# The second reading's range check on ScalarE instead of VectorE, in a linear-attention and SiLU kernel

## The chip, the cores and the metric

The kernel runs on one core of a Trainium2 chip, in one launch. The metric is device time in microseconds. The engines are named as in the profile: PE (TensorE, with PEld for its weight loads), DVE (VectorE), ACT (ScalarE), POOL (GpSimd) and SP (SyncE, which here only issues transfers).

## The reference

A gated recurrence over 768 tokens, for 4 batches and 8 heads of dimension 48, feeds a two-layer network with SiLU over 3072 tokens (384 to 2048 to 384):

```python
for t in range(S):
    state = alpha[:, :, t, :, None] * state + np.einsum('bhd,bhe->bhde', k[:, :, t], v[:, :, t])
    y[:, :, t] = np.einsum('bhd,bhde->bhe', q[:, :, t], state)
x = y.transpose(0, 2, 1, 3).reshape(B * S, H * D)
h = x @ w_in
out = (h * (1.0 / (1.0 + np.exp(-h)))) @ w_out
```

The two weight matrices arrive in 8-byte floats (the code tests for it with `wide`), everything else in 4-byte floats.

## The kernel before, in words

The work is in `quotients` (line 356). It takes the recurrence in 24 chunks of 128 tokens (`NT`, one batch and one stretch of tokens each) and handles it by products and quotients of the gates, which holds only while the numbers stay within a range. So it also checks its inputs. If the check fails, the program runs `general` instead (line 20), which is written at the end behind a branch (line 1267); with the inputs measured here that branch isn't taken.

**Steps and slots.** The loop at line 1185 makes 25 steps of four slots. In a slot one stage of the attention is issued: from step 8 on, slot 0 has `land` and `scores` of the chunk before (`n = step - 1`), slot 1 `products` and slot 2 `quotient` of the current one, slot 3 `values`, `states` and `flip` of the one before. After each stage `fill(step, slot)` (line 1166) issues pieces of the network by due times: `marks` names the slots at which phases of the piece list begin and end, and `fill` issues pieces until the work due by then is done. What is left after the loop is issued one piece after the other.

**Pieces.** `enter_plain` (line 897, first two groups of four chunks) makes one ps_m bank by twelve matmuls and a Silu on ACT. `enter` (line 917, the four other groups) makes the first layer by a scheme of 20 products for each of two column halves, in seven pieces; each product goes to one of three ps_m banks, and each bank is read by a copy on ACT (line 936) or a sum on DVE (line 944) before it is written again. One of the copies' targets, `part`, has a single buffer that DVE reads. `leave` (line 1021) makes the second layer in seven products of two ps_o banks, read by ACT copies (lines 1040, 1059, 1064) and DVE sums (lines 1042, 1074, 1085). From the third group on, a piece of `leave` of one group alternates with a piece of `enter` of the next. At the start of each such group `sums_x` (line 878) makes eleven sums on DVE.

**Order.** A scheduler orders each engine's instructions at build time; a call of `keep_in_program_order` pins an instruction behind the one traced just before it on its engine. PE's are all pinned from the step at which the weights have been converted. The order on the chip is then fixed, and each engine works through its queue in order, with semaphores where another engine or a transfer must be awaited.

**The check.** The weights and alpha are read a second time, for their range. `audit` (line 657) is a generator over 37 pieces: 9 of alpha (128 x 1024 floats, 512 KB), 12 of w_in (128 x 512 doubles, 512 KB) and 16 of w_out (128 x 384 doubles, 384 KB). For each it issues a transfer from SP's queue (lines 675, 677) into the single buffer `bits`, and at its next call reduces it on DVE (line 685): the largest magnitude of alpha, the largest and the smallest magnitude of the weights' upper words, 65 reduces in all. `fill` calls it in every second slot from step 15 on (line 1178); the loop at line 1215 calls it for the rest, between the last pieces. Then lines 1220 to 1239 turn the collected maxima and minima into one flag, which each engine loads.

Of the kernel before, what the change touches and what calls it, by code (L numbers as in the profile page):

```python
# [8 lines left out]
F32 = mybir.dt.float32  # L9
I32 = mybir.dt.int32  # L10
U32 = mybir.dt.uint32
U8 = mybir.dt.uint8
AF = mybir.ActivationFunctionType
ALU = mybir.AluOpType
E = mybir.EngineType
AX = mybir.AxisListType.X
# [3 lines left out]
def general(  # L20
# [89 lines left out]
    for i, L in enumerate(LEVELS):  # L110
        top = work.tile([128, 128], I32, name="top")
        dve.tensor_single_scalar(top, xor, i, ALU.logical_shift_right)
        right = top.rearrange("p (b two l) -> p b two l", two=2, l=L)[:, :, 1, :]
        m = masks[L] = consts.tile([128, NP, 64], U8, name=f"mask{L}")
        for j in range(NP):
# [18 lines left out]
    def weights():  # L134
# [8 lines left out]
        for dst, src in pieces:  # L143
# [15 lines left out]
            m = gpool.tile([128, 512], F32, name="g")[:, 0:n]  # L159
            act.activation(m, top, AF.Copy, bias=1.0, scale=2.0**-20)  # L160
            dve.scalar_tensor_tensor(m, lo, 2.0**-52, m, ALU.mult, ALU.add)
# [116 lines left out]
    def moe(ci):  # L278
# [3 lines left out]
        for f in range(NFT):  # L282
# [4 lines left out]
            gf = gpool.tile([128, B * C], F32, name="g")  # L287
            act.activation(gf, ps, AF.Silu)
            gs.append(gf)
# [66 lines left out]
def quotients(  # L356
# [19 lines left out]
    nc = tc.nc  # L376
    dve, act, gps = nc.vector, nc.scalar, nc.gpsimd
# [16 lines left out]
    B, H, S, D = q.shape  # L394
# [3 lines left out]
    HD = H * D  # L398
    DF = moe_w_in.shape[1]
    NKT = HD // 128  # L400
    NFT = DF // 128
# [3 lines left out]
    GB = 4  # L405
# [6 lines left out]
    def pool(name, bufs=1, space=None):  # L412
        kw = {} if space is None else {"space": space}
        return ctx.enter_context(tc.tile_pool(name=name, bufs=bufs, **kw))

    PS = bass.MemoryType.PSUM
    consts = pool("consts")
    fix = pool("fix")
# [21 lines left out]
    dve.memset(table, 0.0)  # L440
    act.activation(table, table, AF.Silu)
    ident = consts.tile([128, 128], F32, name="ident")
# [64 lines left out]
    wide = moe_w_in.dtype != F32  # L507
    pieces_in = [(t, c) for c in range(0, DF, 512) for t in range(NKT)]
    sources = [moe_w_in[t * 128 : t * 128 + 128, c : c + 512] for t, c in pieces_in]
# [44 lines left out]
    earlier, later = [(low, 0), (high, 1)], [(low, 1), (high, 0)]  # L554
    ones = consts.tile([128, 1], F32, name="ones")
    gps.memset(ones, 1.0)

    st = [fix.tile([128, NP, 2, D], F32, name=f"st{b}") for b in range(B)]
    for t in st:
# [54 lines left out]
    def weights(which):  # L614
# [9 lines left out]
        def rounding(bits):  # L624
# [3 lines left out]
            tc.keep_in_program_order(  # L628
                act.activation(up, bits.bitcast(U32)[:, :, 0], AF.Copy, scale=2.0**-29))
            return up  # L630
# [21 lines left out]


    AW = 1024
    seen = []

    def audit():


        flat = alpha.rearrange("b h s d -> (b h s d)").rearrange("(p c) -> p c", p=128)  # L660
        todo = [(flat[:, c : c + AW], AW, 0) for c in range(0, flat.shape[1], AW)]
        if wide:
            todo += [(moe_w_in[t * 128 : t * 128 + 128, c : c + 512], 512, 1)
                     for c in range(0, DF, 512) for t in range(NKT)]
            todo += [(moe_w_out[f * 128 : f * 128 + 128, :], HD, 1) for f in range(NFT)]
        for kind in (0, 1):
            n = sum(x[2] == kind for x in todo)
            if n:
                seen.append([fix.tile([128, n], F32, name=f"seen{kind}{i}") for i in range(2)])
        at = [0, 0]  # L670
        for src, n, kind in todo:
            t = late["look"].tile([128, 512, 2], I32, name="bits")
            if kind == 0:
                x = t.rearrange("p n w -> p (n w)")[:, 0:n].bitcast(F32)
                nc.sync.dma_start(x, src)
            else:
                nc.sync.dma_start(t[:, 0:n, :].rearrange("p n w -> p (n w)"), src.bitcast(I32))
                x = t[:, 0:n, 1]
            yield
            i = at[kind]  # L680
            at[kind] += 1
            for which, op in ((0, ALU.max), (1, ALU.min)):
                if kind == 1 or which == 0:
                    tc.keep_in_program_order(
                        dve.tensor_reduce(seen[kind][which][:, i : i + 1], x, axis=AX, op=op,  # L685
                                          apply_absolute_value=True))

    xts, xcs = {}, {}

# [207 lines left out]
    def enter_plain(grp, h, pair):  # L897
# [4 lines left out]
        for f in range(8 * pair, 8 * pair + 8, 2):  # L902
# [5 lines left out]
            q, i = divmod(f, 4)  # L908
            act.activation(gts[grp, h, pair][:, i : i + 2, q % 2, :], ps, AF.Silu)  # L909
            if grp == 1 and pair == h == 0:  # L910
# [6 lines left out]
    def enter(grp, pair):  # L917
# [21 lines left out]
        def silu(h, i):  # L939
            x = halves[h][:, i : i + 2]  # L940
            act.activation(x, x, AF.Silu)  # L941

# [156 lines left out]
    def convert(which, upto):  # L1099
        while conv_done[which] < min(upto, n_conv[which]):  # L1100
            next(conv[which], None)
            conv_done[which] += 1
# [38 lines left out]
    def go_on():  # L1141

        nonlocal done
        next(pieces[done][0], None)
        done += 1

    audits = audit()
    done, bridged = 0, 0
    STEPS = NT + 1
# [16 lines left out]
    def fill(step, slot):  # L1166

        at = step * SLOTS + slot
        if at < marks[0]:
            if at == SLOTS:  # L1170
                next(conv[0])
            elif step >= 1:
                convert(0, (at - SLOTS) * 3 // (marks[0] - SLOTS) + 1)
            return
        i = next(i for i, m in enumerate(marks[1:]) if at < m)
        a, b = [work_at[n] for n in ([0] + phases)[i : i + 2]]
        due = a + (b - a) * (at - marks[i] + 1) / (marks[i + 1] - marks[i])
        if at % 2 == 0 and step > 3 * GB + 2:
            next(audits, None)
        while work_at[done + 1] <= due and pieces[done][2] <= bridged:  # L1180
            convert(0, 3 * (done // 2) + 6)
            convert(1, 3 * (done - 6) // 2)
            go_on()

    for step in range(STEPS):
        if step == 1:
            load(NIN)
        stages = [[(scores, 1)], [(products, 0)], [(values, 1)], [(states, 1)]]
        if step == 1:

            stages = stages[1::-1] + stages[2:]
        elif step >= NA:
            stages = [[(land, 1), (scores, 1)], [(products, 0)], [(quotient, 0)],
                      [(values, 1), (states, 1), (flip, 0)]]
        for slot, group in enumerate(stages):
            for stage, lag in group:
                n = step - lag
                if not 0 <= n < NT:
                    continue
                stage(n)  # L1200
                if stage is values:
                    bridged = n + 1
                if stage is states and n + 1 + NIN < NA:
                    load(n + 1 + NIN)
                if stage is states and n + NV < NT:
                    load_v(n + NV)
            if step * SLOTS + slot == (NA + 1) * SLOTS - 1:
                x = decayed.rearrange("p (o i c) -> p o i c", o=2, c=C)
                for r, o in later:
                    gps.memset(x[r, o, :, 0:CH], 0.0)  # L1210
            fill(step, slot)
            if step * SLOTS + slot >= NA * SLOTS - 1 and conv_done[1] == NFT and not late:
                settle()
    turns = 0
    while next(audits, 0) is None:
        turns += 1
        for _ in range(1 + turns % 2):
            go_on()

    checks = [(least.rearrange("p n j -> p (n j)"), ALU.min, 2.0**-64, ALU.is_gt),  # L1220
              (seen[0][0], ALU.max, 1.0, ALU.is_le)]
    if wide:
        checks += [(seen[1][0], ALU.max, float(1083 << 20), ALU.is_le),
                   (seen[1][1], ALU.min, float(898 << 20), ALU.is_ge)]
    ends = work.tile([128, len(checks)], F32, name="ends")
    for i, (x, op, bound, holds) in enumerate(checks):
        e = ends[:, i : i + 1]
# [21 lines left out]
@with_exitstack  # L1249
def kernel(  # L1250
    ctx: ExitStack,
    tc: tile.TileContext,
    q: bass.AP,
    k: bass.AP,
    v: bass.AP,
    alpha: bass.AP,
    moe_w_in: bass.AP,
    moe_w_out: bass.AP,
    out: bass.AP,
):  # L1260


    flag = ctx.enter_context(tc.tile_pool(name="flag", bufs=1))
    small = flag.tile([1, 1], I32, name="small")
    args = (q, k, v, alpha, moe_w_in, moe_w_out, out)
    within = quotients(tc, small, *args)
    with tc.If(within < 1, label="general"):
        general(tc, *args)
# [30 lines left out]
```

## Time and profile before

| | |
|---|---|
| median of three runs | 560.08 us (558.29, 560.08, 560.13) |
| span of the profiled execution | 558.1 us |
| mean granted TensorE clock | 0.994 |
| reduces of the check (L685) | 65, 42.5 us of DVE, first at 247.2 us, last at 518.4 us |
| transfers of the check | 37, 17.2 MB, the first of them issued at 95.3 us, the others from 248.7 to 514.8 us |
| loading of the flag (L1239) | at 527 us on four engines, at 531.8 us on PE |

The span runs from the first to the last instruction of one profiled execution; the page gives no other time for it. Busy times are shares of that span. A row of the page's fifth part names line, engine and operation, then what is written from what is read, the number of instructions, busy time and the mean of one, and last the engine's idle time just before them and what ended it. In the timeline each row has its start and its duration in us, and in brackets the idle time before it. A matmul of 4-byte floats leaves two records, so that one product of `enter` has four.

### The profile page before, as it was taken

Reading aid. Unit: us, or ns where it says so; the run is one execution under the profiler, and the core shown is the slowest. Engines: PE = TensorE matmul, PEld = TensorE weight load, DVE = VectorE, ACT = ScalarE, POOL = GpSimd, SP = SyncE. Lnnn points to the kernel's source line nnn. Section 1 sums busy time; section 2 is a strip of 40 time slices with the busy share of each in tenths; the row PEclk is TensorE's granted clock in tenths of the full one; section 3 lists DMA queues with packets and bytes.
Section 4 is the critical chain, followed back from the end, with each engine's and each line's share of the span. In section 5 each row is a group of like instructions: output and inputs, shape, how many; then the busy total and the mean of one; then the engine's idle time right before and its main releaser. Section 6 shows DMA issues by size and latency. Waiting matters only on the chain. (4 is left out here: it accounts for less than half of the span.)

```text
span 558.1 us, 12640 instructions
## 1 busy us (share of the span) xinstructions
PE 541.4 (97%) x5026; PEld 488.8 (88%) x5026; DVE 445.1 (80%) x801; ACT 208.4 (37%) x466; POOL 75.9 (14%) x146
## 2 busy tenths in 40 slices
PE   5999999999999999999999999999999999999996
PEld 3788887998899898899999999988998999998996
DVE  5887889974999799997998986998894775857531
ACT  3456643223333243353353353353263341432200
POOL 4100010221211211021021021021121000001000
PEclk9799999999999999999999999999999999999999
DMA  9999861164445525355445654717712122333101
GB/s 218 255 276 177 232 189 40 38 164 108 126 131 136 142 62 134 88 145 157 129 109 142 194 141 115 198 22 179 180 48 84 53 99 95 111 109 106 38 25 32
DMA packets 99220, 70.13 MB, mean 126 GB/s; under 512 B 56272, under 2 KB 88656, under 8 KB 99152
## 3 DMA queue, kind: packets, MB, share of 16 engines
q1 hardware_dynamic: 97232, 65.30, 44.6%
q0 software_dynamic: 1920, 3.93, 2.0%
q8 instruction: 41, 0.67, 0.5%
q14 instruction: 27, 0.22, 0.1%
HBM read 61.34 MB, written 7.86 MB: 124 GB/s over the span
## 5 line engine op out<-in xcount | busy, mean ns | idle before, releaser
L388 PE MATMUL ps_o<-w_out,g 128*128 128x192 f32 x768 | 134.7, 329 | 1.1 <-DVE o L1042 0.9
L388 PEld LDWEIGHTS ps_o<-w_out,g 128*128 128x128 f32 x768 | 125.4, 190 | 5.1 <-DVE o L1042 2.3
L388 PE MATMUL ps_m<-xt,w_in 128*128 128x256 f32 x480 | 113.6, 383 | 1.5 <-ACT xt L851 1.1
L388 PEld LDWEIGHTS ps_m<-xt,w_in 128*128 128x128 f32 x480 | 89.1, 190 | 14.4 <-ACT xt L851 1.6
L388 PE MATMUL ps_o<-wt,g 128*128 128x192 f32 x576 | 99.7, 326 | 0.0
L388 PEld LDWEIGHTS ps_o<-wt,g 128*128 128x128 f32 x576 | 95.1, 190 | 1.6 <-issue 0.2
L388 PE MATMUL ps_m<-xc,w_in 128*128 128x256 f32 x288 | 70.7, 382 | 0.0
L685 DVE TENSOR_REDUCE seen<-bits 128x1 f32<-128x384 int32 (+2 forms) x65 | 42.5, 689 | 24.0 <-DMA bits<-in_moe_w_out_dram 19.6
L388 PEld LDWEIGHTS ps_m<-xc,w_in 128*128 128x128 f32 x288 | 53.6, 190 | 7.0 <-DVE g L944 0.3
L941 ACT ACTIVATE g<-g 128x1024 f32<-128x1024 f32 x32 | 33.0, 1056 | 59.0 <-DVE g L944 59.0
L1033 DVE TENSOR_TENSOR g<-g 128x512 f32<-128x512 f32 x72 | 49.8, 708 | 6.1 <-PE ps_o L388 6.1
L1045 POOL DMA_DIRECT2D out_dram<-o x40 | 22.0, 550 | 223.2 <-DVE o L1042 127.6
L813 POOL TENSOR_SCALAR_AFFINE_SELECT g<-g 64x256 f32<-64x256 f32 x64 | 34.2, 534 | 124.8 <-ACT g L806 105.8
L388 PE MATMUL ps_m<-xc,wx 128*128 128x256 f32 x192 | 50.0, 383 | 1.0 <-DVE xc L586 1.0
L936 ACT COPY g<-ps_m 128x512 f32<-128x512 f32 x64 | 36.5, 588 | 36.5 <-PE ps_m L388 36.4
L388 PEld LDWEIGHTS ps_m<-xc,wx 128*128 128x128 f32 x192 | 35.2, 190 | 5.3 <-ACT u L1064 1.3
L944 DVE TENSOR_TENSOR g<-ps_m,g 128x512 f32<-128x512 f32 x56 | 37.0, 684 | 2.9 <-PE ps_m L388 2.7
L722 DVE TENSOR_TENSOR_SCAN u<-al,one 128x516 f32<-128x516 f32 x24 | 30.0, 1249 | 10.6 <-ACT al L719 10.3
L909 ACT ACTIVATE g<-ps_m 128x512 f32<-128x512 f32 x32 | 19.1, 596 | 42.8 <-PE ps_m L388 42.3
L936 ACT COPY part<-ps_m 128x512 f32<-128x512 f32 x32 | 18.9, 589 | 43.0 <-DVE g L944 21.3
L752 DVE TENSOR_TENSOR_SCAN p<-al,inv 128x516 f32<-128x516 f32 x24 | 29.9, 1246 | 1.0 <-PE ps_a L388 0.4
L388 PE MATMUL ps_a<-g,vn 128*32 128x128 f32 x768 | 27.5, 278 | 1.8 <-POOL g L801 1.7
(126 smaller groups left out, 611.4 us busy)
## 6 DMA issues: line engine op xcount, KB each, us to landing
bits<-in_moe_w_in_dram SPq DMA_DIRECT2D x24, 512.0 KB, 4.8
bits<-in_moe_w_out_dram SPq DMA_DIRECT2D x32, 384.0 KB, 3.1
at<-in_alpha_dram SPq DMA_DIRECT2D x64, 96.0 KB, 2.5
kt<-in_k_dram SPq DMA_DIRECT2D x64, 96.0 KB, 2.5
qt<-in_q_dram SPq DMA_DIRECT2D x64, 96.0 KB, 2.6
bits<-in_alpha_dram SPq DMA_DIRECT2D x9, 512.0 KB, 3.8
out_dram<-o POOLq DMA_DIRECT2D x40, 96.0 KB, 2.4
flips<-turn SPq DMA_DIRECT2D x12, 256.0 KB, 2.4
```

The source lines that it names most:

```text
L388: in_order(nc.tensor.matmul(*args, **kw))
L685: dve.tensor_reduce(seen[kind][which][:, i : i + 1], x, axis=AX, op=op, apply_absolute_value=True))
L722: dve.tensor_tensor_scan(u[:, end - 1 :: -1], sg[:, end:0:-1], one[:, end:0:-1], 0.0, ALU.mult, ALU.add)
L752: dve.tensor_tensor_scan(p[:, 0:end], sg[:, 0:end], iv[:, 0:end], 0.0, ALU.mult, ALU.add)
L813: gps.affine_select(x, x, pattern=[[0, NP], [1, CH]], compare_op=ALU.is_ge, fill=0.0, base=0, channel_multiplier=-1)
L909: act.activation(gts[grp, h, pair][:, i : i + 2, q % 2, :], ps, AF.Silu)
L936: act.copy(to, ps)
L941: act.activation(x, x, AF.Silu)
L944: dve.tensor_tensor(to, a, b, op)
L1033: dve.tensor_tensor(cells(grp, h, pair, *to), cells(grp, h, pair, *x), cells(grp, h, pair, *y), ALU.subtract)
L1045: (gps if grp < NG - 1 else nc.sync).dma_start(out[r : r + C, c * HO : (c + 1) * HO], o)
```

## The change

The check's arithmetic goes from DVE to ACT, its transfers go from SP's queue to ACT's, and its calls begin with step 10 and come twice in each slot: once before the slot's pieces and once after them. Each piece takes two calls. In the first (after the slot's pieces) Abs is made of the piece that was fetched; for a weight it reads the uppermost two bytes of each double as an integer. In the second (before the next slot's pieces) Relu is made of what exceeds the bound and is summed along the row into one column of `beyond`; for a weight another Abs stands ahead of it. Then the next transfer is issued. All of these are pinned in program order, and the buffer stays single. With two calls a slot the generator ends within the steps, so that the loop over the rest has nothing to do, and the flag is formed from `beyond` right after the last step.

```diff
+    minus = consts.tile([128, 1], F32, name="minus")
+    gps.memset(minus, -1.0)
...
     AW = 1024
-    seen = []
+    audited = [(0, c, AW) for c in range(0, B * H * S * D // 128, AW)]
+    if wide:
+        audited += [(1, src, src.shape[1]) for src in list(sources)]
+    beyond = fix.tile([128, len(audited)], F32, name="beyond")
 
     def audit():
         flat = alpha.rearrange("b h s d -> (b h s d)").rearrange("(p c) -> p c", p=128)
-        todo = [(flat[:, c : c + AW], AW, 0) for c in range(0, flat.shape[1], AW)]
...
-        for src, n, kind in todo:
+
+        def step(to, x, func, scale=1.0, bias=0.0, to_sum=None):
+            kw = {} if to_sum is None else {"accum_out": to_sum}
+            tc.keep_in_program_order(act.activation(to, x, func, bias=bias, scale=scale, **kw))
+
+        def begin(kind, src, n):
             t = late["look"].tile([128, 512, 2], I32, name="bits")
+            words = t.rearrange("p n w -> p (n w)")
+            to, src = (words[:, 0:n].bitcast(F32), flat[:, src : src + n]) if kind == 0 else (
+                words[:, 0 : 2 * n], src.bitcast(I32))
+            tc.keep_in_program_order(act.dma_start(to, src))
+            return t
+
+        t = begin(*audited[0])
+        yield
+        for i, (kind, _, n) in enumerate(audited):
+            x = t.bitcast(F32)
+            x = x.rearrange("p n w -> p (n w)")[:, 0:n] if kind == 0 else x[:, 0:n, 0]
             if kind == 0:
-                x = t.rearrange("p n w -> p (n w)")[:, 0:n].bitcast(F32)
-                nc.sync.dma_start(x, src)
+                step(x, x, AF.Abs)
             else:
-                nc.sync.dma_start(t[:, 0:n, :].rearrange("p n w -> p (n w)"), src.bitcast(I32))
-                x = t[:, 0:n, 1]
+                step(x, t.bitcast(I16)[:, 0:n, 3], AF.Abs, scale=2.0**-14)
             yield
-            i = at[kind]
-            at[kind] += 1
-            for which, op in ((0, ALU.max), (1, ALU.min)):
-                if kind == 1 or which == 0:
-                    tc.keep_in_program_order(
-                        dve.tensor_reduce(seen[kind][which][:, i : i + 1], x, axis=AX, op=op,
-                                          apply_absolute_value=True))
+            if kind == 1:
+                step(x, x, AF.Abs, scale=-1.0, bias=ones)
+            step(x, x, AF.Relu, scale=1.0 if kind == 0 else 2.0**14 / 944, bias=minus,
+                 to_sum=beyond[:, i : i + 1])
+            if i + 1 < len(audited):
+                t = begin(*audited[i + 1])
+            yield
...
-        if at % 2 == 0 and step > 3 * GB + 2:
+        if step > 2 * GB + 1:
             next(audits, None)
         while work_at[done + 1] <= due and pieces[done][2] <= bridged:
             convert(0, 3 * (done // 2) + 6)
             convert(1, 3 * (done - 6) // 2)
             go_on()
+        if step > 2 * GB + 1:
+            next(audits, None)
...
-              (seen[0][0], ALU.max, 1.0, ALU.is_le)]
-    if wide:
-        checks += [(seen[1][0], ALU.max, float(1083 << 20), ALU.is_le),
-                   (seen[1][1], ALU.min, float(898 << 20), ALU.is_ge)]
+              (beyond, ALU.max, 0.0, ALU.is_le)]
```

More of the change, by code (lines that the diff above doesn't have):

```diff
@@ L12 @@
 U8 = mybir.dt.uint8
+I16 = mybir.dt.int16
 AF = mybir.ActivationFunctionType
@@ L654, in quotients @@
     AW = 1024
-    seen = []
+    audited = [(0, c, AW) for c in range(0, B * H * S * D // 128, AW)]
+    if wide:
+        audited += [(1, src, src.shape[1]) for src in list(sources)]
+    beyond = fix.tile([128, len(audited)], F32, name="beyond")
     def audit():
         flat = alpha.rearrange("b h s d -> (b h s d)").rearrange("(p c) -> p c", p=128)
-        todo = [(flat[:, c : c + AW], AW, 0) for c in range(0, flat.shape[1], AW)]
-        if wide:
[L663 to L670, printed above, removed]
-        for src, n, kind in todo:
-            t = late["look"].tile([128, 512, 2], I32, name="bits")
+        def step(to, x, func, scale=1.0, bias=0.0, to_sum=None):
+            kw = {} if to_sum is None else {"accum_out": to_sum}
+            tc.keep_in_program_order(act.activation(to, x, func, bias=bias, scale=scale, **kw))
+        def begin(kind, src, n):
+            t = late["look"].tile([128, 512, 2], I32, name="bits")
+            words = t.rearrange("p n w -> p (n w)")
[8 more added lines that the diff above has]
+            x = x.rearrange("p n w -> p (n w)")[:, 0:n] if kind == 0 else x[:, 0:n, 0]
@@ L1220, in quotients @@
     checks = [(least.rearrange("p n j -> p (n j)"), ALU.min, 2.0**-64, ALU.is_gt),
-              (seen[0][0], ALU.max, 1.0, ALU.is_le)]
-    if wide:
-        checks += [(seen[1][0], ALU.max, float(1083 << 20), ALU.is_le),
-                   (seen[1][1], ALU.min, float(898 << 20), ALU.is_ge)]
+              (beyond, ALU.max, 0.0, ALU.is_le)]
     ends = work.tile([128, len(checks)], F32, name="ends")
```

## The prediction

> **What bounds the kernel now.** I read the page's busy times and slices first, then the waits, then busy time by stretch, then the timeline.
>
> ```profile
> span 558.1 us, 12640 instructions
> PE 541.4 (97%) x5026; PEld 488.8 (88%) x5026; DVE 445.1 (80%) x801; ACT 208.4 (37%) x466; POOL 75.9 (14%) x146
> PE   5999999999999999999999999999999999999996
> DVE  5887889974999799997998986998894775857531
> ACT  3456643223333243353353353353263341432200
> L685 DVE TENSOR_REDUCE seen<-bits 128x1 f32<-128x384 int32 (+2 forms) x65 | 42.5, 689 | 24.0 <-DMA bits<-in_moe_w_out_dram 19.6
> ```
>
> PE never rests except in the first and last slices. The range check costs DVE 42.5 us of work and 24.0 us of waiting, but DVE isn't what sets the end: what it gives up is worth only the PE gaps that it causes.
>
> ```profile
> 144.00:188.00 44.00, 44.00 (x476) 39.85 (x479) 40.41 (x74) 13.66 (x42) 9.17 (x16) 1.00 0.53 143
> 188.00:240.00 52.00, 50.65 (x577) 45.62 (x569) 50.76 (x99) 21.09 (x54) 7.71 (x15) 1.00 0.39 102
> 240.00:325.00 85.00, 85.00 (x872) 78.14 (x871) 78.17 (x128) 36.40 (x85) 13.23 (x26) 1.00 0.52 142
> ```
>
> These are the stretches that take the new work (stretch and its length, then busy us and instructions of PE, PEld, DVE, ACT, POOL). The code makes two calls per slot from step 10; 37 pieces need 75 calls, so the check runs from slot 40 to slot 77. In the trace the score matmuls start step 10 at 143.9 us and step 19 at 320.5 us. A slot lasts 4.05 us up to 188 us (16.2 us a step), then about 5.35. ACT is busy 71.2 of 181 us there; DVE has 1.2 us to spare in 52 from 188 to 240, where no check runs yet.
>
> ```profile
> 237.42 1.99 PE L388 MATMUL ps_m<-xc,w_in 128*128 128x256 f32 x8
> ...
> 240.22 1.08 ACT L936 COPY g<-ps_m 128x512 f32<-128x512 f32 x2
> ...
> 242.71 1.03 PE L388 MATMUL ps_m<-xc,wx 128*128 128x256 f32 x4
> ...
> 243.78 0.59 ACT L936 COPY part<-ps_m 128x512 f32<-128x512 f32 x1 [0.55 <-PE ps_m L388]
> ...
> 247.90 1.89 PE L388 MATMUL ps_m<-xc,w_in 128*128 128x256 f32 x8
> ```
>
> This shows how late ACT may be. Three ps_m banks go round. The bank written at 242.71 is copied at 243.78 and free at 244.37, and written again at 247.90: 3.5 us to spare. The one written at 237.42 is copied only at 240.22 (the scores' copies and L824 are ahead in ACT's queue), free at 240.81, rewritten at 242.71: 1.9 us to spare. Putting each copy of the eight entry blocks beside the next write of its bank, I find 1.7 to 2.7 us to spare in most cases for the six copies of pieces 1 and 2 of seven, and some 3.5 us or more later.
>
> **What the Trainium skill says.** "ScalarE: Activation LUTs", section "Table sets: the hidden batching unit", says that relu, copy and abs are in every set; so Abs and Relu between Silus need no table load. The trace has one load (1.28 us) for Copy and Silu together, and no Abs or Relu. The same page, "What ACT_TABLE_LOAD costs", puts an ACTIVATE at 186 ns + 0.833 ns an element, and 93 ns more for a bias given as a column; the trace agrees: 588 ns for 512 elements (L936; 613 by the formula), 1056 for 1024 (L941; 1039). "DMA: Bandwidth & Descriptors", "Issuing engines are not separate DMA queues": queues share the same DMA engines, so ACT's own queue saves only issue time, here 327 ns a piece on SP.
>
> **The change, part by part.**
>
> *Reduces leave DVE* (-42.5 us of DVE). What that is worth on PE:
>
> ```profile
> 513.75 1.00 DVE L685 TENSOR_REDUCE seen<-bits 128x1 f32<-128x384 int32 x2
> ...
> 515.68 0.76 PE L388 MATMUL ps_o<-w_out,g 128*128 128x192 f32 x3 [0.71 <-DVE o L1042]
> ```
>
> Two reduces stand ahead of the sum (L1042) that PE waits for: 0.71 us. The other gap of size after 240 us is 1.02 us at 368.7, behind an xc sum (L586), with 1.2 us of reduces at 356.8 ahead of it in a DVE queue that hardly rests in between; with two gaps of 0.12 and 0.07 the sum is **-1.9 us**. Bounds: 0 (something else is next) and -3, if the matmul starts also close up a little inside stretches shown as busy.
>
> *Transfers leave SP* (37 x 0.33 = 12 us of issue, and 85 us of SP waiting for reduces). Behind them stand the a, k, q loads and the flips; the only wait on such a load is 1.5 us of DVE, once, not on PE. Nothing, at most -1.
>
> *ACT's new work.* Alpha, 9 pieces: Abs 1.06 (row L941) and Relu with a column bias 1.15 = 2.21 us. w_in, 12: the nearest strided read is L629 at 686 ns for 512 elements; 0.69 + 0.78 + 0.78 = 2.25. w_out, 16: L629 at 564 ns for 384; 0.56 + 0.65 + 0.65 = 1.87. Sum 19.9 + 27.0 + 29.9 = 76.8 us, and 37 issues of 0.33 = 12.2: 89 us; ACTs in a row start some 0.1 us before the end of the last (240.22 to 241.18: 0.48 us apart at 0.59 each), so about 79. Reading out the accumulator isn't in the trace: 0 to 0.2 us each (the smallest ACT row takes 0.2), so 0 to 7; I take 0. ACT goes from 71 to 150 busy us of 181 (83%), before any wait.
>
> *The added wait.* A piece's Abs waits for its transfer with all later ACT work queued behind it: bank copies, which PE needs, and the part copies, which DVE needs.
>
> ```profile
> bits<-in_moe_w_in_dram SPq DMA_DIRECT2D x24, 512.0 KB, 4.8
> bits<-in_moe_w_out_dram SPq DMA_DIRECT2D x32, 384.0 KB, 3.1
> ...
> bits<-in_alpha_dram SPq DMA_DIRECT2D x9, 512.0 KB, 3.8
> ```
>
> Landing takes 3.1 to 4.8 us; the slot's pieces between issue and Abs fill 4 to 5.35. DVE, in the same position now, waited 24.0 us in 18 times, 1.3 each. I take 0.65, bounds 0 and 1.3.
>
> *What PE feels.* The slot's last Abs and the next slot's Abs, Relu and issue stand side by side on ACT, except where scores or values come between. One block is 2.25 + 0.33 - 0.2 = 2.4 us for w_in and 1.87 + 0.33 - 0.2 = 2.0 for w_out; with the wait 3.05 and 2.65. Where 3.5 us are to spare nothing shows; where 1.8 are, in 2 of 7 pieces (0.29), PE stalls 1.25 and 0.85. Entry blocks begin at about 190 us (slot 52), so 9 w_in and 16 w_out pieces meet them: 9 x 0.29 x 1.25 + 16 x 0.29 x 0.85 = 3.3 + 3.9 = **+7.2 us**. The alpha pieces and three of w_in lie beside plain pieces, each of which uses one bank for twelve matmuls of 0.216 us from start to start, 2.6 us, so that two others pass before a bank comes up again: over 4 us to spare after its Silu. 0; without that cover their blocks would cost as w_in's do. Bounds: wait 0 gives 9 x 0.29 x 0.6 + 16 x 0.29 x 0.2 = 2.5; wait 1.3 gives 5.0 + 7.0, and 9 x 0.71 x 0.2 = 1.3 in the other pieces: 13.3.
>
> *The end.* The verdict is taken once the steps are over instead of at 527 us; its DVE operations are under 1.5 us in all and PE's read of the flag took 0.48 at 531.8 without a PE gap. 0, from -0.2 to +1.
>
> Sum: 558.1 - 1.9 + 7.2 = 563.4. The page gives the span only; the runs shown were 558.29, 560.08 and 560.13, so the median lies 2.0 above the span. **565.4 us**; own range 561 to 572.
>
> **Rivals.**
> *ACT's idle time takes it all* (not slower). For it: ACT idles 110 us in these stretches, 59 us of all its idling is waiting for DVE (first line below), which gets quicker, and placement may put the blocks into those waits. Against: the order is fixed, and DVE at 98% from 188 to 240 gets no relief there. It decides if a block with its wait stays under 1.8 us where copies are late. 558.1 - 1.9 + 2.0 = 558.2; 556 to 562.
>
> ```profile
> ACT g L941 <- DVE g L944: 59.0, 16, 6.4
> ...
> DVE seen L685 <- DMA bits<-in_moe_w_out_dram: 19.6, 14, 2.5
> ...
> DVE seen L685 <- DMA bits<-in_moe_w_in_dram: 4.4, 4, 1.5
> ```
>
> *ACT sets the pace.* One buffer makes a serial loop: block, landing, block. It takes 2.4 + 3.8 + 0.1 = 6.3 us for alpha, 7.3 for w_in, 5.2 for w_out. If one piece per slot really binds, slots stretch: 9 x 2.25 + 3 x 3.25 + 9 x 1.95 + 0 = 47 us, giving 605; the compiler may let the check slip against the pieces, so half: 584 (572 to 606). Against it: nothing forces later copies to stay behind a waiting Abs at build time.
>
> *It isn't what it says:* a table load for each function after all, two at 1.28 us per piece, 95 us: 650.
>
> **Chances.** Forecast 0.54 (of it 0.08 below 562.9), ACT absorbs 0.30 (0.06 of it below 557.3), ACT paces 0.14, table loads 0.02. Half a per cent, 2.8 us, is about what a measurement can tell from no change. Faster 0.06; same 0.24 + 0.08 = 0.32; slower 0.62. Range 557.5 to 582: it leaves out the fast tail (0.06) and most of the pacing case (0.12).
>
> **What would show it.** Right: no new table load; ACT near 280 to 290 us busy; new PE gaps of about 1 us between 190 and 330 us released by ACT copies or by DVE sums that wait for copies; the gaps at 368 and 515 gone; ACT waits for the new transfers under 1.3 us each. Wrong if PE shows no more gaps than now (ACT absorbed it), or if slots between 144 and 240 us stretch by 2 us each (ACT paces).

## The result and the profile after

| | before | after |
|---|---|---|
| median | 559.84 us (558.29 to 560.13) | 598.21 us (596.54 to 599.78) |
| ratio, with its 95% interval | | 1.0688 [1.0662, 1.0715] |
| span of the profiled execution | 558.1 us | 598.0 us |
| mean granted TensorE clock | 0.994 | 0.971 |

The change makes the kernel 6.9% slower; the prediction had 565.4 us and a range up to 582. Span, engines, three rows of slices (PE, ACT, PEclk) and the row of the check, from the page of the changed kernel:

```profile
span 598.0 us, 12667 instructions
PE 555.5 (93%) x5026; PEld 498.1 (83%) x5026; DVE 410.7 (69%) x732; ACT 272.6 (46%) x589; POOL 76.3 (13%) x147
PE   6999999999979769979988989999999999999996
...
ACT  3565653223556465576667555335343342332100
PEclk9999999999979779979999998999999999999999
L668 ACT ACTIVATE bits<-bits 128x384 f32<-128x384 int16 (+2 forms) x33 | 24.0, 728 | 65.1 <-DMA bits<-in_moe_w_out_dram 26.9
```

PE has the same 5026 matmul records. Its idle time went from 558.1 - 541.4 = 16.7 us to 598.0 - 555.5 = 42.5, and the matmuls themselves take 14.1 us longer: 25.8 + 14.1 = 39.9, the whole difference of the spans. The PE row now has holes in slices 12 to 24, just where ACT is fuller, and the PEclk row has its 7s there too. And ACT, which is busy for less than half of the span, stands idle for 65.1 us ahead of the check's first Abs. From slice 26 on the rows of PE and PEclk are as before: the loss is local.

Busy time by stretch of the changed kernel (stretch and length, then busy us and instructions of PE, PEld, DVE, ACT, POOL, then granted clock, DMA share, GB/s). The bounds are the score matmuls that open steps 10, 13, 15 and 19, except that two of step 15's 32 score matmuls run at 256.40 already, ahead of a gap of 3.21 us, so that this gap counts to the second stretch:

```profile
142.30:205.10 62.80, 54.17 (x568) 48.28 (x568) 45.77 (x85) 32.85 (x68) 8.70 (x16) 0.89 0.63 172
205.10:260.00 54.90, 45.95 (x435) 40.11 (x434) 43.90 (x85) 33.17 (x72) 6.59 (x12) 0.93 0.59 167
260.00:357.70 97.70, 89.09 (x863) 79.19 (x863) 70.75 (x121) 63.12 (x145) 12.49 (x24) 0.97 0.55 158
357.70:598.00 240.30, 232.16 (x1763) 215.65 (x1762) 138.36 (x245) 81.27 (x172) 24.31 (x44) 0.99 0.14 38
```

The same steps of the kernel before:

```profile
143.90:192.50 48.60, 48.60 (x569) 44.16 (x570) 44.45 (x83) 14.53 (x43) 9.17 (x16) 1.00 0.53 140
192.50:236.60 44.10, 42.75 (x435) 38.38 (x435) 43.50 (x84) 17.54 (x41) 6.21 (x12) 1.00 0.36 96
236.60:320.50 83.90, 83.90 (x865) 77.08 (x864) 78.00 (x129) 35.35 (x82) 12.23 (x24) 1.00 0.53 146
320.50:558.10 237.60, 230.89 (x1763) 214.20 (x1762) 167.61 (x310) 78.80 (x167) 24.59 (x44) 1.00 0.34 96
```

So the three stretches with the check lose 14.2, 10.8 and 13.8 us, together 38.8, and the fourth 2.7. Step by step the ten steps from 10 to 19 took 198.0 us and now take 240.7, 42.7 more; what comes ahead of them and after them is 1.6 and 1.2 us shorter. ACT is busy for only 52 to 65% of the three stretches. It isn't full; it is waiting.

What ACT waits for between 140 and 362 us in the changed kernel (us in total, times, longest):

```profile
ACT bits L668 <- DMA bits<-in_moe_w_out_dram: 26.9, 14, 3.5
ACT bits L668 <- DMA bits<-in_alpha_dram: 21.2, 8, 3.9
ACT bits L668 <- DMA bits<-in_moe_w_in_dram: 16.9, 8, 3.9
```

Thirty waits for a landing, 65.0 us in all, 2.2 each. PE's four largest waits in the same stretch:

```profile
PE ps_m L389 <- ACT g L944: 7.5, 2, 4.7
PE ps_m L389 <- ACT g L917: 4.2, 1, 4.2
PE ps_m L389 <- ACT part L944: 4.0, 6, 1.7
PE ps_a L389 <- DMA kn<-flips: 4.0, 1, 4.0
```

With the smaller rows it waits for 28.4 us: 20.5 are put down to ACT, 3.9 to sums of DVE, 4.0 to a load of the flips. How ACT's waits reach PE is seen around one of them. From the timeline of the changed kernel (start, duration, in brackets the idle time before and what ended it):

```profile
165.64 0.33 ACTq L675 DMA_DIRECT2D bits<-in_alpha_dram  x1
...
166.91 1.17 ACT L832 ACTIVATE st<-st,least 128x96 f32<-128x96 f32 x4
170.70 1.06 ACT L668 ACTIVATE bits<-bits 128x1024 f32<-128x1024 f32 x1 [2.62 <-DMA bits<-in_alpha_dram]
...
171.78 0.60 ACT L917 ACTIVATE g<-ps_m 128x512 f32<-128x512 f32 x1
...
172.43 1.65 PE L389 MATMUL ps_m<-xt,w_in 128*128 128x256 f32 x3 [4.15 <-ACT g L917]
```

The transfer begins at 165.64 and lands five microseconds later. ACT has nothing else ahead of the Abs after 168.1, so it stands for 2.62 us. The Silu that empties the bank PE needs (L917) is queued behind the Abs. PE has stopped at 168.28 and starts again at 172.43. This is a plain piece (six products, which leave twelve records), where the prediction put the cost at zero.

One thing of the change was misread in the prediction: the second reading now takes 33 pieces, not 37. The change builds its list from `sources`, and four entries of w_in have been taken from that list by then, by the fetches that run ahead. So there are 9 pieces of alpha, 8 of w_in and 16 of w_out (HBM reads 61.34 MB before, 59.24 after), and the other four of w_in aren't checked.

### The profile page after: what moved, and what is told of

The parts are those of the page before. It is cut to its first block, busy times and chain, and to the rows that moved or that the text cites. A ratio compares the mean times of both kernels' runs of the same rounds, so it can differ in the third digit from the quotient of the medians.

```text
span 598.0 us, 12667 instructions
## 1 busy us (share of the span) xinstructions
PE 555.5 (93%) x5026; PEld 498.1 (83%) x5026; DVE 410.7 (69%) x732; ACT 272.6 (46%) x589; POOL 76.3 (13%) x147
## 3 DMA queue, kind: packets, MB, share of 16 engines
HBM read 59.24 MB, written 7.86 MB: 112 GB/s over the span
## 5 line engine op out<-in xcount | busy, mean ns | idle before, releaser
L389 PEld LDWEIGHTS ps_o<-w_out,g 128*128 128x128 f32 x768 | 127.6, 192 | 5.3 <-ACT g L949 1.7
L389 PE MATMUL ps_m<-xt,w_in 128*128 128x256 f32 x480 | 116.2, 389 | 6.4 <-ACT g L917 4.2
L389 PEld LDWEIGHTS ps_m<-xt,w_in 128*128 128x128 f32 x480 | 90.5, 193 | 21.0 <-ACT g L917 4.4
L389 PE MATMUL ps_m<-xc,w_in 128*128 128x256 f32 x288 | 74.4, 396 | 0.0
L389 PE MATMUL ps_m<-xc,wx 128*128 128x256 f32 x192 | 53.3, 402 | 10.4 <-ACT g L944 7.5
L389 PEld LDWEIGHTS ps_m<-xc,w_in 128*128 128x128 f32 x288 | 55.9, 198 | 7.6 <-issue 0.2
L668 ACT ACTIVATE bits<-bits 128x384 f32<-128x384 int16 (+2 forms) x33 | 24.0, 728 | 65.1 <-DMA bits<-in_moe_w_out_dram 26.9
L389 PEld LDWEIGHTS ps_m<-xc,wx 128*128 128x128 f32 x192 | 36.9, 201 | 17.6 <-ACT g L944 8.0
L949 ACT ACTIVATE g<-g 128x1024 f32<-128x1024 f32 x32 | 32.9, 1053 | 35.9 <-DVE g L952 35.4
L952 DVE TENSOR_TENSOR g<-g,part 128x512 f32<-128x512 f32 x24 | 16.5, 686 | 30.8 <-ACT part L944 20.9
L389 PEld LDWEIGHTS ps_a<-p,kp 48*64 48x64 f32 (+1 forms) x640 | 21.4, 149 | 15.2 <-issue 7.9
L389 PE MATMUL ps_a<-p,kp 48*64 48x64 f32 (+2 forms) x640 | 26.4, 263 | 7.4 <-ACT xt L859 3.4
L917 ACT ACTIVATE g<-ps_m 128x512 f32<-128x512 f32 x32 | 18.9, 594 | 29.3 <-PE ps_m L389 28.4
```

The source lines that it names most:

```text
L389: in_order(nc.tensor.matmul(*args, **kw))
L668: tc.keep_in_program_order(act.activation(to, x, func, bias=bias, scale=scale, **kw))
L952: dve.tensor_tensor(to, a, b, op)
```

## The experiments

**Theory: one serial loop.** With a single buffer the order is: block on ACT, transfer, landing, block on ACT. ACT can't pass a waiting Abs, so when one piece per slot is called for, the loop is longer than the slot and everything that PE needs of ACT falls behind. **Rivals:** ACT's added work (some 79 us) is what delays the copies; the check's transfers, now crowded into 210 us, delay the loads that attention needs; the transfers on ACT's queue hold up SP.

### The work alone, and the wait alone

*The work alone* (e4_work_only): all of ACT's new operations, at the same places, on a resident tile; no transfer.

```diff
-            t = late["look"].tile([128, 512, 2], I32, name="bits")
+            t = late["bits"]
...
-            tc.keep_in_program_order(act.dma_start(to, src))
```

> All of ScalarE's range-check arithmetic stays where the change puts it, but it works on one resident tile and the 33 transfers are left out, so that nothing is awaited (the data are thus not checked). If the wait for the landing, with ScalarE's queue behind it, is the cause: 558 to 567 us. If ScalarE's added work alone is the cause: 585 us or more. If the transfers' traffic is the cause: 558 to 567 us as well.

Measured: 559.90 us, ratio to before 0.9975 [0.9966, 0.9984]; span 557.4 us. The engines, from its page:

```profile
PE 539.6 (97%) x5026; PEld 487.1 (87%) x5026; DVE 411.7 (74%) x732; ACT 271.1 (49%) x589; POOL 78.8 (14%) x148
```

ACT is as busy as in the change (271.1 us against 272.6) and DVE as light, and PE is as dense as before. So the work costs nothing that shows; together with DVE's relief and the missing transfers it is worth 0.25%, 1.4 us.

*The wait alone* (e3_wait_only): the transfers stay whole, the arithmetic is done on 8 columns of each piece.

```diff
+            m = 8
+            x = x[:, 0:m]
...
-                step(x, t.bitcast(I16)[:, 0:n, 3], AF.Abs, scale=2.0**-14)
+                step(x, t.bitcast(I16)[:, 0:m, 3], AF.Abs, scale=2.0**-14)
```

> All 33 transfers and the waits for them stay, but Abs and Relu take 8 columns instead of 384 to 1024 (only those are checked). If the wait for the landing is the cause, most of the loss stays: 580 to 598 us. If the added ScalarE work is the cause: 558 to 567 us. If both are needed together: 567 to 580 us.

Measured: 592.12 us, 1.0567 [1.0537, 1.0598]. ACT is busy for 230.3 us only. PE's largest wait between 140 and 362 us:

```profile
PE ps_a L389 <- DMA kn<-flips: 11.5, 3, 5.9
```

With most of the arithmetic gone, ACT only waits longer: 33.5 us for w_out, 30.9 for alpha, 26.1 for w_in, together 90.5 in 33 waits. 5.7 of the 6.9% remain. Work and wait can't be added up: without most of the work the wait gets longer. But PE's gaps have a second releaser here, the landing of `kn<-flips`, a load on SP's queue that attention needs. So the traffic and SP's queue had to be tried by themselves.

### The traffic

*Halves from SP, arithmetic on other data* (e5_traffic_no_wait): each piece is fetched in two halves from SP's queue, and ACT works on a tile that lies there already, so it waits for nothing.

```diff
-            tc.keep_in_program_order(act.dma_start(to, src))
-            return t
+            for e in range(2):
+                m = n // 2
+                to, x = ...
+                nc.sync.dma_start(to, x)
+            return late["still"]
```

> The same bytes are moved at the same points of the program, by SyncE's queue and in halves into a smaller buffer that nobody reads; ScalarE does its arithmetic on a resident tile (the data are thus not checked). Traffic and ScalarE work stay, the wait of ScalarE for the landing goes. If that wait is the cause: 558 to 568 us. If the traffic slows the loads and the flips that the steps need: 580 us or more. If the added work is the cause: 585 us or more.

Measured: 583.66 us, 1.0418 [1.0369, 1.0467], in the range named for the traffic. But this isn't a test of the traffic alone: with one buffer each half has to wait on SP for the last one to land. From SP's and PE's waits of this kernel:

```profile
SPq L677 <- DMA bits<-in_moe_w_out_dram: 30.6, 28, 2.6
```

```profile
PE ps_a L389 <- DMA kn<-flips: 17.4, 5, 6.8
```

With w_in (23.8 us) and alpha (15.1) SP waits 69.5 us for its own halves. I had moved the serial loop to SP, not removed it; what stands behind it there is the load of the flips.

*The same traffic without the loop* (e6_traffic_dram): every piece is copied, from ACT's queue as in the change, into a DRAM tile of its own that nobody reads; ACT works on a resident tile.

```diff
-            t = late["look"].tile([128, 512, 2], I32, name="bits")
+            t = aside.tile([128, 512, 2], I32, name=f"aside{len(made)}")
...
-            return t
+            return late["bits"]
```

> ScalarE's arithmetic on a resident tile as in the run with the work alone (559.9 us), and the 33 transfers of the change at their places on ScalarE's queue, each into a memory tile of its own in DRAM, so that neither ScalarE nor the queue waits for one to land (the data are thus not checked). The traffic is there in full. If the wait for the landing is the cause of nearly all: 560 to 568 us, some us over the work alone. If the traffic, which delays the flips and the loads, is the cause of a good part: 575 us or more.

Measured: 565.71 us, 1.0066 [1.0036, 1.0097]. Work and traffic together cost 0.7%, that is 0.9% more than the work alone. PE's only waits of size on this kernel's loads are two for the flips, 3.9 us in all. SP's own transfers wait 43.0 us, in 18 waits, for the landing of these copies, though nobody reads what they write; more on this below. The target is DRAM, so the bytes take another way than in the change; as a size for the traffic it is a stand-in.

### Whose queue, whose engine

*The transfers on SP's queue* (e7_sp_queue), otherwise the change:

```diff
-            tc.keep_in_program_order(act.dma_start(to, src))
+            nc.sync.dma_start(to, src)
```

> The change with one part undone: the transfers are issued on SyncE's queue again. ScalarE still waits for the landing. If the wait is the cause: 590 to 605 us, as the change or more, since SyncE now waits with its loads queued behind for ScalarE's last read of the buffer. If sharing of the queues (flips beside check transfers) matters more: 575 to 590 us.

Measured: 599.03 us, 1.0669 [1.0634, 1.0704]: no different from the change. ACT waits for landings as long (63.1 us), while PE's gaps have another releaser: 28.9 us in 7 for `kn<-flips`, which now stand on SP behind transfers that wait for ACT to empty the buffer.

*DVE's reduces with the change's calls* (e9_dve_calls): the kernel before, with its reduces and its transfers from SP, but two calls in each slot from step 10.

```diff
+            yield
...
-        if at % 2 == 0 and step > 3 * GB + 2:
+        if step > 2 * GB + 1:
             next(audits, None)
...
+        if step > 2 * GB + 1:
+            next(audits, None)
```

> The kernel before with the change's calls alone: reduces on VectorE and SyncE's queue as before, but begun from step 10, the transfer issued before a slot's pieces and reduced after them. If a wait for the landing in any engine's ordered queue is the cause, it is as slow as the change or slower, VectorE having less idle time: 595 us or more. If it is ScalarE that can't wait: 560 to 575 us.

Measured: 599.50 us, 1.0658 [1.0614, 1.0703]. With no instruction of the check on ACT the kernel loses the same 6.6%. The road isn't the one I had in mind, though. DVE waits for landings only 15.1 us between 140 and 362. Who waits on PE and on SP in that stretch:

```profile
PE ps_a L388 <- DMA kn<-flips: 30.9, 8, 6.8
```

```profile
SPq L677 <- DVE seen L685: 29.6, 16, 7.4
```

Here the loop's waiting is done by SP: the next transfer waits there for the reduce of the last piece, with the flips behind it (29.6 us for weights, 14.6 for alpha). Three kernels with two calls a slot, one buffer and the whole check (the change, e7, e9) come out between 1.066 and 1.069; the engine and the queue only decide by which way the waiting reaches PE.

*The wait with no transfer* (e12_pool_wait): in place of the transfer GpSimd writes the buffer four times, some 4 us in all. ACT waits as in the change, nothing is fetched, and SP has no part in it.

```diff
-            tc.keep_in_program_order(act.dma_start(to, src))
+            for _ in range(4):
+                tc.keep_in_program_order(gps.memset(words.bitcast(F32), 1.0))
```

> The change with its 33 transfers replaced by four fills each of the same buffer on GpSimd, about 3.8 us in all by the 0.95 us of one such fill (the data are thus not checked). ScalarE waits as long as for a landing, but nothing is transferred and SyncE has no check transfer to wait for. If ScalarE's wait with its queue behind it is enough: 585 us or more. If most of the loss comes by way of SyncE, whose loads and flips wait for the check's transfers: 560 to 570 us.

Measured: 596.25 us, 1.0629 [1.0606, 1.0651]. Waits of ACT and of PE between 140 and 362 us:

```profile
ACT bits L668 <- POOL bits L676: 78.2, 31, 4.1
```

```profile
PE ps_m L389 <- ACT g L945: 8.1, 4, 3.7
PE ps_a L389 <- ACT xt L860: 4.7, 3, 2.0
```

ACT's waiting, without the check's traffic and without SP, is enough for a loss of nearly this size, and most of PE's gaps come from ACT's copies, none from loads. Two things keep the sizes from being the same: ACT waits longer than in the change (78.2 us against 65.0), and GpSimd's own mask (L822) comes late behind its fills, so that PE waits 3.5 us for it.

### The length and the frequency of the loop

*A shorter landing* (e13_short): the transfers bring 16 of 128 partitions; ACT works on the whole tile, which lies there.

```diff
-            tc.keep_in_program_order(act.dma_start(to, src))
+            tc.keep_in_program_order(act.dma_start(to[0:16], src[0:16]))
```

> The change with each transfer cut to 16 of the 128 partitions (the others are not checked); ScalarE's work and the wait stay, the landing gets shorter, some 2.4 us by the 64 to 96 KB transfers of the profile. If the loop of block, landing and block sets the pace: 2.4 + 2.4 + 0.1 = 4.9 us against slots of 4.05 and 5.35, so 9 x 0.85 = 8 us and 3 us for w_in in short slots, together 565 to 572 us. If any wait at all costs as much: 585 us or more.

Measured: 565.36 us, 1.0083 [1.0063, 1.0104]. The median landing falls from 3.6 to 4.3 us to 2.2 to 2.6, and with 1.4 to 1.7 us less a piece the loss falls from 6.9 to 0.8%. (An eighth of the bytes is moved, too, but e6 puts all of the traffic at under 1%.) ACT's waits for landings between 140 and 362 us are 17.1 us in 11. So the loss has an edge: where the loop fits into the slot, or its excess into what ACT can slip, PE hardly feels it.

*Only the first call in each slot* (e2_one_call; a piece takes two slots):

```diff
-        if step > 2 * GB + 1:
-            next(audits, None)
```

> The change with the second call of each slot left out, so that a transfer has a whole slot with its attention stage (some 5 us) instead of the slot's pieces alone, and a piece of the check takes two slots. If the time to land decides: between the two runs measured, 562 to 572 us, with waits of ScalarE of under 1 us each. If the halved number of transfers decides: 575 to 580 us, half the loss of the change.

Measured: 562.59 us, 1.0037 [1.0023, 1.0052]. The waits weren't under 1 us each, as expected: ACT still waits 36.5 us for landings, in 18 waits, over half of what it does in the change. That costs PE next to nothing; with two slots for a piece, some 10 us from one to the next, ACT has time to catch up. Waits in themselves aren't the cost; a loop longer than the slot is.

*One call in every second slot* (e2_far): a call makes Abs and Relu of the piece and begins the next transfer, which then has two slots to land.

```diff
             else:
                 step(x, t.bitcast(I16)[:, 0:n, 3], AF.Abs, scale=2.0**-14)
-            yield
...
-        if step > 2 * GB + 1:
+        if at % 2 == 0 and step > 2 * GB + 1:
             next(audits, None)
...
-        if step > 2 * GB + 1:
-            next(audits, None)
```

> The whole check with its arithmetic on ScalarE, but a piece is worked on in one call every second slot: a transfer has two slots, about 10 us, to land instead of the pieces of one slot. If the wait for the landing is the cause: 558 to 567 us, with waits of ScalarE for these transfers near 0. If the added work as such is the cause: 570 to 590 us, since the same work is spread over twice the slots. If the traffic is the cause: about 575 us.

Measured: 562.83 us, 1.0041 [1.0028, 1.0054]. ACT's waits for landings are down to some 9 us. What is left over is on SP's side. From SP's waits of this kernel between 140 and 362 us:

```profile
SPq L487 <- DMA bits<-in_moe_w_in_dram: 15.1, 4, 5.3
```

With alpha and the flips' own loads behind it, 43 us in all: attention's loads on SP stand still until the check's transfers land, though they read and write other tiles.

*The same with the transfers on SP's queue* (e8_far_sp): the edits of e2_far and of e7_sp_queue.

> As the run with one call every second slot (562.8 us), but with the transfers on SyncE's queue, in line with the flips and loads. If what is left of its loss is the flips' landing beside a transfer of the other queue: 559 to 561.5 us. If SyncE's own waiting for ScalarE's last read takes its place: 563 us or more.

Measured: 559.18 us, 0.9962 [0.9953, 0.9970], span 557.8 us, and on its page:

```profile
PE 539.5 (97%) x5026; PEld 488.4 (88%) x5026; DVE 413.7 (74%) x732; ACT 271.5 (49%) x589; POOL 77.5 (14%) x147
```

It is faster than both kernels, by 0.4% than the one before. The waits of attention's loads for the check's transfers are down to 2.7 us between 140 and 362 us, and ACT's waits for landings are 8.6 us in all. SP waits 38.1 us for ACT to empty the buffer, without a gap on PE.

*The same with all 37 pieces* (e10_far_sp_full): the source list in full, so that the four pieces which the change leaves out are read as well.

```diff
-        audited += [(1, src, src.shape[1]) for src in list(sources)]
+        audited += [(1, moe_w_in[t * 128 : t * 128 + 128, c : c + 512], 512) for t, c in pieces_in]
+        audited += [(1, moe_w_out[f * 128 : f * 128 + 128, :], HD) for f in range(NFT)]
```

> The quicker version (one call every second slot, transfers on SyncE's queue, 559.2 us) with the four pieces of w_in put back that the change no longer reads: 37 pieces, the rest of them between the last pieces of the network. If its gain is VectorE's relief: 558.5 to 560 us, still below the kernel before. If it comes from the four pieces left out: 561 us, as the kernel before.

Measured: 559.65 us, 0.9967 [0.9956, 0.9979]. The gain of 0.3% doesn't come from reading less.

## Why the prediction was wrong

**The loop, from the trace.** All 33 transfers of the changed kernel stand in one view, that of line 675 (duration shortest/median/longest in ns, then the first and the last start):

```profile
L675 ACTq DMA_DIRECT2D bits<-in_moe_w_out_dram x16: 334/335/378, 263.2 to 354.5; - x16
L675 ACTq DMA_DIRECT2D bits<-in_alpha_dram x9: 334/334/2238, 144.3 to 200.5; - x9
L675 ACTq DMA_DIRECT2D bits<-in_moe_w_in_dram x8: 334/338/369, 206.4 to 256.5; - x8
...
DMA to landing us min/median/max: 3.0/4.0/6.6
```

From one alpha transfer to the next it is (200.5 - 144.3) / 8 = 7.0 us, of w_in 7.2, of w_out 6.1. Thirty-two turns take 354.5 - 144.3 = 210.2 us. The 32 slots that they belong to, 40 to 72, took 300.0 - 143.9 = 156.1 us in the kernel before: 54 us too few. Of these, ACT gave 18: the check slipped against the attention's slots (the first transfer starts 2.0 us after slot 40 opens, the last 20.4 us after slot 72), nearly all of it within the alpha pieces, 18.1 us by the ninth. From there on the two run in step: 154.0 us for the next 24 turns, 151.7 for the next 24 slots, where the kernel before took 123.7. So 36 us reached PE by slot 72, and 7 more in the two steps in which the slipped pieces run: the 42.7 us of the ten steps.

Point by point:

**"Reduces leave DVE", -1.9.** Right in size: e4, with the work moved and no transfers, gains 0.25%, 1.4 us; e10, with all 37 transfers, gains 0.33%; and the part of the change after step 19 is 1.2 us shorter.

**"ACT's new work".** Right. By the prediction's prices 33 pieces are 67.8 us; by the rows of each shape they are 67.5. The read-out of the sum, taken as 0 with a bound of 7 us, is an instruction of its own, with this row among those by shape:

```profile
L668 ACT ACTIVATION_READ_ACCUMULATOR bits<-bits,minus 128x1 f32 x33 | 6.3, 190 | 0.0
```

Together 73.8 us, of which 64.2 show as busy, since neighbours overlap by about 0.1. There is one table load, as before: the rival "It isn't what it says" is out, and what the Trainium skill says of relu, copy and abs ("ScalarE: Activation LUTs", "Table sets: the hidden batching unit") agrees with this trace.

**"The added wait", 0.65 us, bounds 0 and 1.3.** Measured 2.2 us in 30 of 33. The bound came from DVE's waits in the old kernel, where a piece has two slots, 10 to 11 us, for its round; in the change it has one. A block of 2.4 us and a landing of 3.8 don't fit into a slot of 4.05: the wait had to be over 2 us, from figures that the prediction itself has in its rival "ACT sets the pace".

**"What PE feels", +7.2, bounds 2.5 and 13.3.** This is the step that failed: PE got 25.8 us more of gaps, not 7.2. It laid each block, once, beside the slack of one ps_m bank, as if ACT were on time again at the next. In a loop that is longer than the slot the lateness is carried on: ACT slipped once by some 18 us, and after that nearly all of each turn's excess went to PE: from the ninth alpha piece on, 24 turns took 30.3 us more than their slots had before, and these slots took 28.0 more. So the alpha pieces, put at 0 because plain pieces have over 4 us to spare, weren't covered either (the gap of 4.15 us above is one), and the first stretch lost 14.2 us. e12 shows that ACT's waiting is enough for a loss of this kind without the check's traffic or SP, and e4 that the work without the waiting costs nothing.

**"ACT sets the pace".** The right mechanism, with a chance of 0.14. Its full loop, with the 33 pieces that there are, gives 9 x 2.25 + 3 x 3.25 + 5 x 1.95 + 16 x 0 = 39.8 us and a span of 598 us, the one that was measured; but that is in good part luck, since the turns were taken too short (alpha 6.3 for 7.0, w_out 5.2 for 6.1, so that w_out seemed to fit its slot) and neither the slip nor the slower clock is in it. Landings were 4.2 and 3.6 us in the medians for the 3.8 and 3.1 that it took, and the read-out adds 0.2. Half of it was taken off because "nothing forces later copies to stay behind a waiting Abs at build time". The order as built does put them behind it, and gave way by two pieces only: between two copies of `values` (L859) ACT's trace has three pieces of the check twice where e4's has four. Without the pins on the check's arithmetic the program has the same order on every engine (it was built, not run), so these pins aren't what holds it.

**"Transfers leave SP", 0.** Wrong in kind, and small in the change by what PE shows of it. In 24 places a transfer on SP waited for the landing of one of the check's, 88.1 us in all; the largest of SP's rows for it between 140 and 362 us in the changed kernel:

```profile
SPq L487 <- DMA bits<-in_moe_w_out_dram: 31.2, 9, 5.2
```

These load tiles that the check has nothing to do with (`at`, `kt`, `qt`), and the kernel before has 3.9 us of such waits. In the trace at 163.15 a load of `qt` waits for, and then posts, the very semaphore that ACT's transfer of 159.01 had posted. PE saw at most 4.0 us of it directly, one late landing of the flips. Waits of this kind come to 43 to 47 us in e2_far, e6 and e2_one_call as well, and these lose 0.4 to 0.7%. e2_far against e8_far_sp gives the price at a cadence where ACT's loop doesn't bind: 1.0041 against 0.9962, 0.8%. The Trainium skill's "DMA: Bandwidth & Descriptors" ("Issuing engines are not separate DMA queues"), on which the step leaned, says that a second issuing engine saves issue time only. These runs show no other gain (e7 loses 6.7%, the change 6.9%), and they show that it can also cost.

**"The end", 0.** Right, within the 1.2 us.

**Not in the prediction at all: the clock.** 14.1 of the 39.9 us are matmul time, not gaps. The granted clock right after the gap of 168.28 to 172.43 us, from the changed kernel's trace (stretch, length, PE busy, granted clock, DMA share, GB/s):

```profile
168.28:172.43 4.15, 0.00 (x0) 0.75 0.56 204
172.43:176.43 4.00, 4.00 (x9) 0.50 0.72 195
176.43:180.43 4.00, 4.00 (x97) 0.91 0.63 196
```

PE comes back at a clock of 0.50 and has its full clock again some 5 us later. The mean clocks give about as much, 598.0 x (1 - 0.971) - 558.1 x (1 - 0.994) = 14.0 us, though a part of that falls into the gaps themselves. The Trainium skill's "TensorE: Matmul & The Clock Gate" ("HAM oscillation — how this bites in real kernels") gives the rule "no PE-idle gaps >~3.4µs". Gaps of 4.15, 4.01, 4.68 and 3.21 us are each followed by a clock of 0.50, one of 2.78 and one of 1.74 by 1.00; but one of 1.79 us at 358.1 is followed by 0.50 as well, and in e13 one of 2.98 us by 0.59 over the next 4 us. So the rule fits the three longest gaps, and these shorter ones show that length isn't all of it. Before the change no gap in these stretches lasted over 1.1 us. Across the runs the clock goes with the gaps (e4 0.997, e13 0.992 with no gap over 3.0 us, e12 0.977), but no run changes the one without the other, so that the gaps cause it is read from the order in time, not tested alone.

**What stays open.** How the change's own gaps divide between late copies on ACT and late loads on SP isn't settled by what released them. By the last releaser ACT has most, 20.5 of 28.4 us, and the largest of DVE's (3.2) came after a wait of DVE for a Silu (L949) behind the check on ACT. But PE waits only for what ends last, and in e9, where SP holds the loop, the late flips alone give about the same time. A second buffer in the change's own calls wasn't tried: there is no room for it in the memory beside the other tiles.

The predicted signs told the cases apart. No table load came with the new work, and ACT was busy for 272.6 us, under the 280 to 290 for want of four pieces. But the gaps weren't about 1 us each, ACT's waits weren't under 1.3, and the slots did stretch, by nothing in step 10 and by 1.6 to 2.0 us in steps 11 to 13, which was the sign named for "ACT sets the pace".

## What to carry over to other kernels

Add up block, issue and landing of a single-buffered helper before anything else and hold the sum against the interval at which it is called. If it doesn't fit, the excess of every turn, less one slip, comes out on the engine that needs the waiting one, however idle the waiting one looks; if it does fit, the same work may be free (here 6.9% slower at one piece a slot, 0.4% faster at one in two slots, with the transfers on the queue that had them). When a forecast halves a rival because the order may give way, write down by how much it can give way once, and what it is then.

## What the runs showed of the hardware that I had not expected

- After a PE gap of 3.2 to 4.7 us the granted clock was 0.50 for some 5 us. In sum the matmuls took 14.1 us longer beside 25.8 us more of gaps.
- Transfers on SP's queue waited up to 5.8 us each, 88.1 us in all, for the landing of transfers begun on ACT's queue into an unrelated tile; with those on SP's own queue (e8) such waits of attention's loads were down to 2.7 us.
- The sum of an ACTIVATE is read out by a separate instruction of 190 ns.
- The landing of alpha's 512 KB pieces took 4.2 us in the median beside 3.8 before, that of the check's 384 KB pieces 3.6 beside 2.9. The check ran in other stretches then (its 384 KB pieces at 454 to 515 us), so what makes the difference isn't shown.
